# High halves of the first MLP's first weight block rounded on GpSimd instead of ScalarE

## The chip, the cores and the metric

The kernel runs on one core of a Trainium2 chip. The metric is the device time of one execution in microseconds (us), lower is better. The core has five engines that each work through their own instruction list in order: PE (TensorE, matrix products), DVE (VectorE), ACT (ScalarE), POOL (GpSimd) and SP, which here only issues DMA transfers. An engine that needs another one's result waits on a semaphore.

## The reference

Three layers follow one another. With B = 2, H = 8, S = 768, D = 64:

```python
mask = q_bucket[:, :, :, None] == k_bucket[:, :, None, :]      # 6-bit hash of q @ proj, k @ proj
scores = np.where(mask, scale * q @ k.T, -1e9)
attn = softmax(scores); x = attn @ v                           # attention, to 1536 tokens x 512
g = x @ w_gate; val = x @ w_val                                # first MLP, 512 -> 1536 -> 512
x = (silu(g) * val) @ w_out
h = x @ w_in; solu = h * softmax(h)                            # second MLP, 512 -> 1024 -> 512
out = (solu - mean) / sqrt(var + 1e-6) * g_ln @ w_out
```

The inputs are float64 for the two MLPs' weights (read as pairs of 32-bit words and turned into float32 on the chip) and the result is float32.

## The kernel before

Every matrix product is done in three products of rounded parts: a float32 number is split into a high part (a copy rounded to the matmul format, `hi`, `xh`, `eh`) and a low part (what the rounding left, `lo`, `xl`, `el`), and hi·hi, lo·hi and hi·lo are summed in PSUM.

**Attention** goes over 8 pairs of heads, 12 query slots a pair, 96 slots in all. For each slot PE computes scores (L553), DVE takes row maxima (L563), ACT the exponentials (L577), PE transposes them (L597, L595), ACT rounds the high part out of PSUM (L606), DVE makes the low part (L610), and every three slots PE multiplies with the values (L632, L636, L631). Results leave by ACT (L699, L703, or L689 for the last two), are scaled with reciprocals which POOL widens (L654, tile `wide`) and PE transposes (L665), multiplied on DVE (L714; L694 for the last), and split into `xh` and `xl` on POOL (L717, L720) or, for the last pair, on ACT and DVE (L695, L696). The scratch tiles of this step (`xf`, `low`, `both`, `wide`) live in the pool `xs`, the last SBUF pool that the attention opens.

**First MLP.** The first weight block (`w_gate` and `w_val`, 128 columns each) is brought to float32 during the attention, in `w1f[0]` and `w1f[1]`. L930 to L933, the lines of the change, split it into `hi` and `lo`. `hidden(f, blk)` then runs 24 matmuls of 512 columns per hidden block and token block (L1132); for the very first of them all 16 that use `hi` come first, the 8 that use `lo` after. The following weight blocks go through `conversions()` (L56, L58, L60, L66 or L55, L68 on DVE and ACT, then L1061 and L967), whose first five steps are traced ahead of the first matmul. 

**What sets the order.** Within the attention, and again from L1182 on, the order on each engine is the order of the code (`manual_schedule`). The lines in between, L886 to L933, are outside both: a planner places each of them in its engine's list when, by its own estimate, what it depends on is done. The planner also interleaves the two hand-ordered parts, so that matmuls of the first MLP stand in PE's list between those of the attention's last slots. The order it arrives at is fixed in the program; on the chip an engine never skips ahead in it.

**The column of ones.** `small` is a tile of 480 bytes per partition at the upper end of SBUF. Its columns hold `gl` (loaded by DMA, L888), `half` and `unit1` (memsets on DVE, L886 and L887). It is opened after the attention's pools are closed and takes memory from them: it lies at bytes 228864 to 229343 of a partition, and `wide` lies at 227616 to 229151. In the kernel before, the first users of `unit1` are the roundings of the second MLP (L1021).

Of the kernel before, what the change touches and what calls it, by code (L numbers as in the profile page):

```python
# [21 lines left out]
P = 128  # L22
# [49 lines left out]
def hash_attention_then_two_mlps(  # L72
# [16 lines left out]
    nc = tc.nc  # L89
    B, H, S, D = q.shape  # L90
    NB = proj.shape[1]
    NT, DM = out.shape
# [58 lines left out]
    w1f = [const.tile([P, DM], F32, name=f"w1f{n}") for n in range(2)]  # L151
# [724 lines left out]
    gl, half, unit1 = small[:, :KF2], small[:, KF2:KF2 + 1], small[:, KF2 + 1:KF2 + 2]  # L876
# [31 lines left out]
    with ExitStack() as m1:  # L908
# [16 lines left out]
        def weights1(f):  # L925
            hi, lo = halves(ws)
            w1_of[f] = [x.rearrange("p n (k f) -> p n k f", k=KD) for x in (hi, lo)]
            return hi, lo

        hi, lo = weights1(0)  # L930
        for n in range(2):
            nc.scalar.copy(hi[:, n], w1f[n])
            nc.gpsimd.tensor_sub(lo[:, n], w1f[n], hi[:, n].bitcast(F32))  # L933

        pieces = []
# [576 lines left out]
```

## Time and profile before

| | us |
|---|---|
| median of 3 runs | 669.58 |
| lowest, highest | 669.57, 669.98 |
| the profiled execution, its own time | 670.97 |
| its span, first to last instruction | 669.1 |
| PE busy in the span | 661.4 |
| DVE, ACT, POOL busy | 530.7, 371.5, 215.4 |

The span is 1.87 us shorter than the profiled execution's own time. "Busy" counts instructions of an engine, not its waits; "[0.56 <-DVE el L610]" behind a row of a timeline says that the engine stood idle for 0.56 us before it, until DVE's instruction of line 610 that writes `el` was done. A busy PE overlaps: a matmul's duration is longer than the distance to the next one.

### The profile page before, as it was taken

What the parts mean: (1) busy time and instruction counts of PE and PEld (TensorE: products, weight loads), DVE (VectorE), ACT (ScalarE), POOL (GpSimd) and SP (SyncE); (2) the same over time, 40 slices, a digit from 0 to 9 for tenths busy, and PEclk for the clock granted to TensorE, in tenths of its full rate; (3) what the DMA queues carried; (4) which work ended last, traced back from release to release, by engine and by line L of the source; (5) the groups of instructions that cost most, each with busy time, mean ns of one, the idle gap of its engine ahead of it and who ended that gap; (6) DMA issues with size and microseconds to landing.
All of it is one profiled execution on the core that took longest, in us unless ns stands there. A gap on an engine that the chain in (4) does not pass through costs nothing.

```text
span 669.1 us, 10300 instructions
## 1 busy us (share of the span) xinstructions
PE 661.4 (99%) x3653; PEld 578.0 (86%) x3653; DVE 530.7 (79%) x912; ACT 371.5 (56%) x754; POOL 215.4 (32%) x247
## 2 busy tenths in 40 slices
PE   8999999999999999999999999999999999999998
PEld 6999999999999988888888888888888888888887
DVE  7888899999999978957877968858974979865781
ACT  7897998989989944644234234224143533342432
POOL 6647666666626330000000000000000575776200
PEclk9999999999999999999999999999999999999999
DMA  6674754746434123351131543213014220212201
GB/s 188 171 191 118 200 147 106 184 123 168 95 93 142 48 64 119 133 189 63 64 125 64 206 171 90 99 64 119 8 63 154 71 92 36 86 69 96 94 17 48
DMA packets 39347, 73.19 MB, mean 109 GB/s; under 512 B 5336, under 2 KB 26904, under 8 KB 38528
## 3 DMA queue, kind: packets, MB, share of 16 engines
q1 hardware_dynamic: 39296, 72.53, 35.8%
q8 instruction: 29, 0.48, 0.3%
q14 instruction: 22, 0.18, 0.1%
HBM read 40.90 MB, written 7.34 MB: 72 GB/s over the span
## 4 chain that ended last, share of the span: by engine, by line
PE 93%; ACT 3%; DMA 1%; DVE 1%; issue 1%; SPq 0%; ACTq 0%; DVEq 0%
PE h L1132 29%; PE s L553 9%; PE h L1262 8%; PE t L597 5%; PE y L1160 5%; PE y L1159 5%; PE y L1158 5%; PE av L632 4%; PE av L636 4%; PE o L1374 3%; PE o L1376 3%; PE o L1375 3%; PE pp L514 2%; PE pp L475 2%; PE t L1355 1%; PE t L595 1%
## 5 line engine op out<-in xcount | busy, mean ns | idle before, releaser
L610 DVE SCALAR_TENSOR_TENSOR el<-t,eh 128x384 fp32r<-128x384 f32 x192 | 97.6, 550 | 19.1 <-ACT eh L606 18.3
L1132 PE MATMUL h<-xh,hi 128*128 128x512 f32 x288 | 112.2, 390 | 0.0
L1132 PE MATMUL h<-xl,hi 128*128 128x512 f32 x288 | 112.1, 389 | 0.0
L1132 PE MATMUL h<-xh,lo 128*128 128x512 f32 x288 | 111.2, 389 | 0.0
L606 ACT CAST eh<-t 128x384 fp32r<-128x384 f32 x192 | 84.7, 499 | 19.3 <-PE t L597 18.8
L1088 POOL TENSOR_TENSOR sf<-yh 128x256 f32<-128x256 f32 x5 | 3.7, 737 | 277.7 <-ACT yh L1173 277.7
L563 DVE TENSOR_REDUCE top<-s 128x1 f32<-128x770 f32 x96 | 90.7, 945 | 1.0 <-PE s L553 0.8
L632 PE MATMUL av<-eh,vs 128*128 128x384 f32 x186 | 64.6, 347 | 0.1
L1132 PEld LDWEIGHTS h<-xh,hi 128*128 128x128 f32 x288 | 54.1, 188 | 11.3 <-DVE sg L1142 0.2
L1132 PEld LDWEIGHTS h<-xl,hi 128*128 128x128 f32 x288 | 54.1, 188 | 11.2
L1132 PEld LDWEIGHTS h<-xh,lo 128*128 128x128 f32 x288 | 54.0, 188 | 11.2
L1142 DVE TENSOR_TENSOR sg<-h,sg 128x512 f32<-128x512 f32 x36 | 24.8, 689 | 43.3 <-PE h L1132 24.0
L553 PE MATMUL s<-ka,qa 128*128 128x384 f32 x192 | 55.1, 368 | 1.4 <-ACT e1f L577 1.2
L1061 ACT CAST hi<-wf 128x1024 fp32r<-128x1024 f32 x17 | 17.9, 1051 | 68.8 <-DVE wf L68 56.8
L1158 PE MATMUL y<-ah,hi 128*128 128x512 f32 x144 | 56.0, 389 | 0.0
L1159 PE MATMUL y<-al,hi 128*128 128x512 f32 x144 | 56.0, 389 | 0.0
L1160 PE MATMUL y<-ah,lo 128*128 128x512 f32 x144 | 56.0, 389 | 0.0
L1144 ACT CAST ah<-sg 128x512 fp32r<-128x512 f32 x36 | 22.4, 622 | 60.0 <-DVE sg L1142 60.0
L636 PE MATMUL av<-el,vs 128*128 128x384 f32 x155 | 52.3, 337 | 0.0
L553 PE MATMUL s<-kb,qb 76*128 76x384 f32 x192 | 49.4, 338 | 0.0
L1170 DVE TENSOR_TENSOR yf<-y,yf 128x512 f32<-128x512 f32 x60 | 40.2, 684 | 4.8 <-PE y L1160 4.5
L632 PEld LDWEIGHTS av<-eh,vs 128*128 128x128 f32 x186 | 35.0, 188 | 0.4 <-ACT both L703 0.4
(295 smaller groups left out, 1612.1 us busy)
## 6 DMA issues: line engine op xcount, KB each, us to landing
raw<-in_moe_w_out_dram SPq DMA_DIRECT2D x10, 1024.0 KB
raw<-in_moe_w_gate_dram SPq DMA_DIRECT2D x12, 512.0 KB
raw<-in_moe_w_val_dram SPq DMA_DIRECT2D x12, 512.0 KB
ka<-kt SPq DMA_DIRECT2D x30, 192.0 KB
raw<-in_moe_w_in_dram SPq DMA_DIRECT2D x4, 1024.0 KB
parked<-raw SPq DMA_DIRECT2D x8, 512.0 KB
moved<-u SPq DMA_DIRECT2D x8, 512.0 KB
v<-in_v_dram SPq DMA_DIRECT2D x8, 384.0 KB
```

Of the source, the lines that this page charges most:

```text
L553: nc.tensor.matmul(s[:, n, :HALF], a[:, rows], m[:, n * HALF:(n + 1) * HALF], start=first, stop=not first,)
L563: bias_of[:] = [nc.vector.tensor_reduce(tops[i % len(tops)], s_of[i][:, :, :HALF + 1], AX.XY, ALU.max, negate=True)]
L606: nc.scalar.copy(half_tile(eh_of, i, g), t_of[i, g])
L610: last_of[i] = nc.vector.scalar_tensor_tensor(half_tile(el_of, i, g), t_of.pop((i, g)), EVEN, half_tile(eh_of, i, g).bitcast(F32), ALU.add ...
L632: nc.tensor.matmul(av, vj[:, c], eh_of[h][:, c, :], start=c == 0, stop=c == C - 1)
L636: nc.tensor.matmul(*low, start=False, stop=False)
L1132: nc.tensor.matmul(ps[n], a[:, n, kk, :], x[:, kk, blk * BLK:(blk + 1) * BLK], start=kk == 0 and a is hi and x is xh, stop=kk == KD - 1 an ...
L1158: nc.tensor.matmul(p, hi[:, cols], ah, start=f == t * FT, stop=False)
L1159: nc.tensor.matmul(p, hi[:, cols], al, start=False, stop=False)
L1160: nc.tensor.matmul(p, lo[:, cols], ah, start=False, stop=f == (t + 1) * FT - 1)
L1170: nc.vector.tensor_add(y, p, y)
L1262: nc.tensor.matmul(dst, a[m](d), w3_of[b][:, l, d], start=start and n == 0, stop=n == 3 * KH - 1, skip_group_check=True,)
```

## The change

The two copies to the rounded format move from ScalarE to GpSimd, as products with a broadcast column of ones. The column is `unit1`.

```diff
         hi, lo = weights1(0)
         for n in range(2):
-            nc.scalar.copy(hi[:, n], w1f[n])
+            nc.gpsimd.tensor_mul(hi[:, n], w1f[n], unit1.to_broadcast([P, DM]))
             nc.gpsimd.tensor_sub(lo[:, n], w1f[n], hi[:, n].bitcast(F32))
```

## Rows read from the trace of the kernel before

**Rows 1.** The page: busy time by engine, and chain that ended last by engine
```profile
PE 661.4 (99%) x3653; PEld 578.0 (86%) x3653; DVE 530.7 (79%) x912; ACT 371.5 (56%) x754; POOL 215.4 (32%) x247
...
PE 93%; ACT 3%; DMA 1%; DVE 1%; issue 1%; SPq 0%; ACTq 0%; DVEq 0%
```

**Rows 2.** Busy time by stretch: length, engines (instructions), granted clock, DMA share, GB/s
```profile
204.00:206.40 2.40, 1.84 (x11) 1.42 (x9) 1.14 (x3) 2.27 (x6) 2.20 (x3) 1.00 0.11 26
206.40:231.00 24.60, 24.59 (x177) 23.80 (x178) 23.95 (x44) 23.19 (x54) 11.88 (x13) 1.00 0.34 111
...
245.73:532.00 286.27, 286.27 (x1264) 236.94 (x1264) 218.91 (x289) 113.51 (x164) 6.39 (x8) 1.00 0.30 103
```

**Rows 3.** The chain in order of time, 228 to 250: start, length, what
```profile
234.18 4.58 PE h L1132 x20
238.76 0.39 PE t L597 x5
...
239.98 0.33 PE pp L665 x3
240.31 2.98 PE h L1132 x13
243.29 0.17 PE t L632
...
245.40 0.33 PE pp L665 x3
245.73 4.36 PE h L1132 x19
```

**Rows 4.** Timeline of ACT: start, length, instruction, idle before it and what ended it
```profile
204.17 1.14 ACT L932 CAST hi<-w1f 128x512 fp32r<-128x512 f32 x2
205.22 0.85 ACT L606 CAST eh<-t 128x384 fp32r<-128x384 f32 x2
...
245.44 0.48 ACT L689 COPY low<-t 64x384 f32<-64x384 f32 x1 [3.52 <-PE t L632]
...
247.72 0.51 ACT L695 CAST xh<-xf 128x384 fp32r<-128x384 f32 x1
```

**Rows 5.** Timeline of PE at 206
```profile
206.34 0.83 PE L597 MATMUL t<-idr,e2r 128*128 128x128 f32 x5 [0.56 <-DVE el L610]
```

**Rows 6.** Timeline of DVE around the attention's end
```profile
233.55 1.03 DVE L610 SCALAR_TENSOR_TENSOR el<-t,eh 128x384 fp32r<-128x384 f32 x2 [0.62 <-ACT eh L606]
234.50 0.89 DVE L645 TENSOR_SCALAR total<-total 128x6 f32<-128x6 f32 x1
...
236.74 1.41 DVE L60 SCALAR_TENSOR_TENSOR wf<-raw,wf 128x1024 int32<-128x1024 int32 x1
...
245.94 0.55 DVE L691 TENSOR_TENSOR xf<-t,low 64x384 f32<-64x384 f32 x1 [2.98 <-ACT low L689]
246.60 0.55 DVE L694 TENSOR_TENSOR xf<-xf,pp 128x384 f32<-128x384 f32 x1
...
249.59 0.55 DVE L696 TENSOR_TENSOR xl<-xf,xh 128x384 fp32r<-128x384 f32 x1
...
250.71 0.06 DVE L887 MEMSET small<- 128x1 f32 x1
```

**Rows 7.** Instructions on the tile small: count, duration ns min/median/max, first and last start
```profile
L888 SPq DMA_DIRECT2D small<-in_moe_g_ln_dram x1: 458/458/458, 241.4 to 241.4; - x1
```

**Rows 8.** POOL's groups, shapes apart: count, busy us, mean ns, idle before them
```profile
L717 POOL TENSOR_TENSOR xh<-xf,one 128x384 fp32r<-128x384 f32 x15 | 12.4, 829 | 26.4 <-DVE top L563 21.9 <-DVE xf L714 4.5
...
L269 POOL TENSOR_TENSOR qs<-q,one 128x768 fp32r<-128x768 f32 x6 | 8.8, 1468 | 0.7 <-DVE top L563 0.7
...
L933 POOL TENSOR_TENSOR lo<-w1f,hi 128x512 fp32r<-128x512 f32 x2 | 2.6, 1290 | 0.2 <-ACT hi L932 0.2
```

**Rows 9.** Instructions on the tile wide: duration ns min/median/max
```profile
L654 POOL TENSOR_TENSOR wide<-one,r x32: 503/507/1482, 45.7 to 237.0; 128x192 f32<-128x192 f32 x32
```

**Rows 10.** Timeline of PE at the start: the seven warming matmuls, and the longest later idle time
```profile
1.22 3.17 PE L399 MATMUL t<-w1f 128*128 128x512 bf16 x7 [1.22 <-DVE w1f L172]
...
11.85 0.62 PE L553 MATMUL s<-ka,qa 128*128 128x384 f32 x2 [0.98 <-ACT e1f L577]
```

## Prediction

> **What bounds the kernel now.** I read the page first: PE is busy 661.4 of 669.1 us and 93% of the chain that ended last is PE [rows 1]. So an edit is worth what it puts into PE's list as idle time, or takes out. Next I read busy time by stretch around the place where the first weight block is used. From 206.40 to 231.00 PE is busy 24.59 of 24.60 us, and from 245.73 to 532.00 all of 286.27 us; in the 2.40 us from 204.00 it is busy 1.84 [rows 2]. Then the chain in order of time shows what fills PE at the seam between attention and first MLP: 20 matmuls of L1132 from 234.18 (4.58 us), then the transposes of the last slot, the spread L665 at 239.98, 13 more of L1132 from 240.31 (2.98 us), then the last product with the values from 243.29, the last spread, and from 245.73 only L1132 [rows 3]. These 33 matmuls, 7.56 us or 0.229 us each, are what keeps PE from waiting while the attention's last slot goes through ACT and DVE. All of them read `hi` or `lo` of the first block, or follow in PE's list matmuls that do.
>
> **The copies that go.** ACT's two casts take 1.14 us at 204.17, and the roundings of a slot (L606) stand behind them at 205.22 [rows 4]. PE then waits 0.56 us for the `el` that follows from these [rows 5]. Without the casts L606 starts about 1.1 us earlier and that wait goes. PE has no other idle time in the 24.6 us after it, so the gain should reach the end: 0.56 us. Its bounds are 0 (if another wait takes its place) and 0.56; I take 0.56.
>
> **The wait that comes.** The new products read `unit1`, and nothing before them did. `unit1` lies in memory that `wide` holds until the spread L665 that ends at 240.31 [rows 3]. So on the chip it can't be written before that matmul, whereas the casts ran at 204. In the trace the memset ran only at 250.71, behind L696, the last instruction that touches any tile of `xs`, which ends at 250.14; DVE had stood idle for 2.98 us before 245.94 [rows 6]. The DMA into another column of the same tile, a neighbour in the code, was issued at 241.4 [rows 7]. I read this so: the semaphores ask only for the tile underneath (the DMA needed no more), but the planner puts the memsets into DVE's list behind the release of the whole pool `xs`. If that is so, the order becomes: all of the attention, L696, memset, product on POOL, first L1132. PE's list can't hold an L1132 ahead of the attention's end, since the first of them needs `hi`, and the 33 covering matmuls move behind it. Queued behind that wait on PE is the whole first MLP.
>
> **The new seam, step by step.** PE has done all that is ready of the attention at 234.18 [rows 3]. The transposes of the last slot need the two L610 that end at 234.58 [rows 6], so they run at about 234.2 to 235.1 instead of 238.6. ACT rounds them by 235.9 (two L606 take 0.85 [rows 4]). DVE then makes the low parts: two L610, 1.03 us. Here I have to choose. DVE's list has L645, L56, L646, L58 and L60 in front of them now, the last of which ends at 238.15 [rows 6]. If L60 stays in front, the low parts run from 238.15 to 239.15; if the last slot overtakes the conversion, from 235.9 to 236.9. I take the first, since L56 to L60 are ready at the same time as before, and keep the second as lower bound. The last product with the values and its spread take 2.44 us (243.29 to 245.73 [rows 3]); begun when the first low part is there, at 238.7, they end at about 241.2. Behind that stands a chain of small steps: L689 0.48 and L695 0.51 on ACT [rows 4], L691, L694 and L696 0.55 each on DVE [rows 6], with some 0.2 us of handing over: 2.85 us, so L696 ends at 244.05. (In the trace it took 4.7, because the first silu and the first weights' low part were in between; neither can be there now.) The two memsets take 0.12: 244.2.
>
> **The product on POOL.** No row shows 512 columns of it. The same operation on 384 columns takes 0.829 us and on 768 columns 1.468 [rows 8]; in between that gives 0.829 + 128 x 0.639/384 = 1.04 us each, and about 0.1 to start. The first L1132 then runs at 245.3. The second product ends at 246.4; PE needs it after 8 matmuls, 1.8 us, so at 247.1: hidden. If the first subtraction (1.29 us [rows 8]) is put between the two products, PE waits some 0.6 us more; I take none. The two subtractions follow until 247.7 and 249.0; PE needs their results after 16 and 20 matmuls, at 249.0 and 249.9: hidden.
> A product on POOL can be held up: one L654 took 1.482 us where the median is 0.507 [rows 9], during a conversion on DVE; L645 took 0.89 us on six columns while POOL worked [rows 6]. I add nothing in the sum, since DVE has nothing of that kind left at 244, and 1.0 us in the upper bound.
> The Trainium skill, page "SBUF — State Buffer", section "SBUF: two separate sides", says that GpSimd and VectorE share one pair of ports as an exclusive lock and that the later one waits out the other's whole instruction. By that the product would start up to one DVE instruction later, and the two long rows agree with it.
>
> **The sum.** Before, PE at 245.73 had the attention and 33 of the matmuls behind it, so the first MLP's work stands as if it had begun without a gap at 245.73 - 7.56 = 238.17. Now it begins at 245.3: +7.1 us. From there on PE is full until 532 [rows 2], and DVE, which starts the next conversions no later against PE's place than before, has no reason to open a gap; so it all arrives at the end. Less 0.56: +6.6 us. Lower bound, the last slot overtaking the conversion: 2.6 us less, +4.0. Upper bound: the remaining conversion steps on DVE and L1061 on ACT standing in the chain of small steps (1.2 us) and POOL held up (1.0): +8.8. The profiled execution took 670.97, so a profiled one after should take 677.6; the median of the runs lies 1.39 below that execution, which gives 676.2, between 673.6 and 678.4.
>
> **The rivals.**
> *The clock falls.* PE would now have nothing from 241.4 to 245.3. The granted clock is 1.00 (2.4 GHz) in every stretch, and the longest idle times are 1.22 at the start and 0.98 later [rows 10], so no row shows what 3.9 us do. What a slow start costs is seen there too: the seven first matmuls, after no earlier work, need 0.43 us for each 512 columns (starts from 1.22 to 3.8) against 0.229, though the clock column gives 1.00 for them. Seven to eight such matmuls cost 1.5 us more: 677.7. Against it speaks that the gap is short.
> The Trainium skill, page "TensorE: Matmul & The Clock Gate", section "HAM oscillation — how this bites in real kernels", has PE fall back to half rate in pauses between bursts; it speaks against this change, and no row here can show it.
>
> *The tile alone holds the memset (not slower).* If the planner goes by `wide` and not by the pool, as the DMA's 241.4 would allow, the spread L665 runs at about 236.2, memset and product follow by 237.4, and L1132 fills PE again while the last slot is on DVE. The same 33 matmuls are then done, only later in the tail, and what is lost is 0.4 us at 234.6 and some 0.2 to 1.2 around 237, less 0.56: 669.6 to 670.6. It decides if the first L1132 starts before PE's last product with the values. For it: the DMA. Against it: the memset at 250.71, after 2.98 idle us on DVE.
>
> *The seam isn't touched.* If the ones were written early after all and the products ran at 204, where POOL is idle a third of the time, only the 0.56 us would be left: 669.0. The shared memory speaks against it.
>
> **How the numbers follow.** About 0.2% (1.3 us) is what a measurement of this kernel can tell from no change. Forecast 676.2: 0.62. Clock falls: 0.20. Tile alone: 0.12. Seam untouched: 0.05. The rest, 0.01, is a gain from a luckier order. Slower by over 0.2%: 0.62 + 0.20 + 0.02 of the tile case = 0.84. Within 0.2%: 0.14. Faster: 0.02. The range takes in the forecast's bounds and the clock case with its upper bound in part, 672.8 to 679.8; the other two, 0.17, are left out.
>
> **What would show it.** The trace after should have L886, L887 right behind L696 on DVE, at about 244; the two products on POOL at about 244.3, not at 204; no L1132 on PE before the last L665; an idle time of 3 to 5 us on PE ahead of the first L1132, ended by POOL `hi`; the transposes of the last slot at 234 to 235; and no 0.56 us wait at 206. It is wrong if L1132 still stands between the last slots on PE, or if PE shows idle time after 246 that isn't there now.

## The result

The changed kernel takes 677.23 us (median of 4 runs, 676.86 to 677.43) against 669.58 (669.33 to 669.98) before: the ratio is 1.0112, with a 95% interval of 1.0097 to 1.0127, so it is slower by 6.5 to 8.5 us. The forecast was 676.2 with a range of 672.8 to 679.8. The profiled execution of the changed kernel took 677.38 us with a span of 675.5.

The list of PE's waits of the changed kernel (us in total, times, longest) has two entries that the kernel before did not have, and the wait at 206 [rows 5] is gone. The long one is the subject here; the short one stands in the last slot, at 234.36:

```profile
PE h L1132 <- POOL hi L932: 5.7, 1, 5.7
...
PE t L632 <- DVE el L610: 0.4, 1, 0.4
```

PE's timeline (start, length, instruction, idle time before it and what ended it) shows the place. The last slot's spread is done, then PE has nothing until the first product of GpSimd is there. And the matmuls that follow start 0.43 us apart, where 0.229 was usual [rows 3]:

```profile
236.60 0.52 PE L665 MATMUL pp<-idr,wide 128*128 128x128 f32 x3
242.84 0.80 PE L1132 MATMUL h<-xh,hi 128*128 128x512 f32 x1 [5.72 <-POOL hi L932]
243.44 0.63 PE L1132 MATMUL h<-xl,hi 128*128 128x512 f32 x1
243.86 0.63 PE L1132 MATMUL h<-xh,hi 128*128 128x512 f32 x1
```

Busy time by stretch (length, then PE, PEld, DVE, ACT and POOL busy with their counts, granted clock, DMA share, GB/s) says why: the clock was granted at half, 1.2 GHz, after PE had stood idle, and for 3.6 us after it had begun again (242.84 to 246.40).

```profile
204.00:206.40 2.40, 2.40 (x19) 2.32 (x18) 2.04 (x4) 2.28 (x6) 2.02 (x2) 1.00 0.05 11
...
240.00:242.00 2.00, 0.00 (x0) 0.00 (x0) 1.08 (x5) 1.46 (x2) 1.15 (x2) 0.50 0.34 67
242.00:244.00 2.00, 1.16 (x3) 0.97 (x4) 0.00 (x0) 1.28 (x1) 2.00 (x3) 0.50 1.09 380
244.00:246.00 2.00, 2.00 (x7) 1.52 (x6) 0.00 (x0) 0.00 (x0) 2.00 (x2) 0.50 0.51 79
...
262.00:532.00 270.00, 270.00 (x1192) 223.64 (x1192) 201.69 (x264) 104.72 (x149) 1.48 (x2) 1.00 0.31 106
```

The first line answers to the 1.84 of 2.40 us before [rows 2]: the wait at 206 has gone. The last shows PE as full as before, so what happens at the seam arrives at the end. The chain in order of time (start, length, what; "issue" pieces left out but one) shows what stands between the last spread, which ends at 237.12, and the first L1132:

```profile
236.46 1.14 DVE wf L60
237.59 0.61 DVE raw L66
...
238.23 0.56 DVE xf L691
...
238.81 0.03 DVE wf L68
238.84 1.11 issue
239.95 0.56 DVE xf L694
...
240.53 0.52 ACT xh L695
...
241.08 0.56 DVE xl L696
241.64 0.01 DVE small L886
241.65 0.03 DVE small L887
...
241.75 1.05 POOL hi L932
...
242.84 19.38 PE h L1132 x77
```

**Where the time went.** The profiled execution of before lost time at its start that the other one did not: PE's last transpose L595 ahead of the copies stands at 203.85 before and at 202.73 after, and up to there the change has touched nothing. (In the experiments below it stands between 202.45 and 203.51.) So 1.12 us of the difference are chance; this is most of the 1.39 us by which the profiled execution of before lay over its median. From that landmark on:

| stretch | before | after | difference |
|---|---|---|---|
| landmark to the next transposes L597 (206.34, 204.47) | 2.49 | 1.74 | -0.75 |
| from there to the end of the values before the last slot (234.18, 231.96) | 27.84 | 27.49 | -0.35 |
| last slot by itself: before 245.73 - 234.18 less 7.56 of L1132; after 231.96 to 237.12 | 3.99 | 5.16 | +1.17 |
| PE idle ahead of L1132 | 0 | 5.72 | +5.72 |
| eight L1132 at half rate: 242.84 to 246.40, less 8 x 0.229 | 0 | 1.73 | +1.73 |

The sum is +7.52; less the chance of 1.12 it is +6.40, and the two profiled executions differ by 6.41. The medians differ by 7.65. Of the 0.35 in the second row, 0.28 belong to the wait at 206 too: its transposes took 0.66 us from L597 to L595 before (206.34 to 207.00) and 0.38 after (204.47 to 204.85). So a wait that the profile shows as 0.56 us cost about 1 us.

### The profile page after: what moved, and what is told of

The parts are those of the page before. It is cut to its first block, busy times and chain, and to the rows that moved or that the text cites. A ratio compares the mean times of both kernels' runs of the same rounds, so it can differ in the third digit from the quotient of the medians.

```text
span 675.5 us, 10299 instructions
## 1 busy us (share of the span) xinstructions
PE 662.5 (98%) x3653; PEld 578.5 (86%) x3653; DVE 530.0 (78%) x912; ACT 371.5 (55%) x752; POOL 218.8 (32%) x249
## 4 chain that ended last, share of the span: by engine, by line
PE 94%; DVE 3%; ACT 1%; issue 1%; DMA 0%; SPq 0%; POOL 0%; DVEq 0%; ACTq 0%
PE h L1132 29%; PE s L553 10%; PE h L1262 8%; PE t L597 6%; PE y L1158 5%; PE y L1160 5%; PE y L1159 5%; PE av L632 5%; PE av L636 4%; PE o L1374 3%; PE o L1376 3%; PE o L1375 3%; PE pp L514 2%; PE pp L475 2%; PE t L1355 1%; PE t L595 1%
## 5 line engine op out<-in xcount | busy, mean ns | idle before, releaser
L1132 PE MATMUL h<-xh,hi 128*128 128x512 f32 x288 | 113.2, 393 | 5.7 <-POOL hi L932 5.7
L1132 PE MATMUL h<-xl,hi 128*128 128x512 f32 x288 | 112.9, 392 | 0.0
L610 DVE SCALAR_TENSOR_TENSOR el<-t,eh 128x384 fp32r<-128x384 f32 x192 | 97.7, 550 | 17.0 <-ACT eh L606 16.1
L1132 PE MATMUL h<-xh,lo 128*128 128x512 f32 x288 | 110.9, 389 | 0.0
L1132 PEld LDWEIGHTS h<-xh,hi 128*128 128x128 f32 x288 | 54.7, 190 | 17.4 <-POOL hi L932 6.0
L1132 PEld LDWEIGHTS h<-xl,hi 128*128 128x128 f32 x288 | 54.6, 190 | 11.3
L1132 PEld LDWEIGHTS h<-xh,lo 128*128 128x128 f32 x288 | 54.1, 188 | 11.3
L553 PEld LDWEIGHTS s<-kb,qb 76*128 76x128 f32 x192 | 34.9, 189 | 0.5 <-DVE kb L441 0.5
```

Of the source, the lines that this page charges most:

```text
L553: nc.tensor.matmul(s[:, n, :HALF], a[:, rows], m[:, n * HALF:(n + 1) * HALF], start=first, stop=not first,)
L610: last_of[i] = nc.vector.scalar_tensor_tensor(half_tile(el_of, i, g), t_of.pop((i, g)), EVEN, half_tile(eh_of, i, g).bitcast(F32), ALU.add ...
L1132: nc.tensor.matmul(ps[n], a[:, n, kk, :], x[:, kk, blk * BLK:(blk + 1) * BLK], start=kk == 0 and a is hi and x is xh, stop=kk == KD - 1 an ...
```

## The experiments

The theory: `unit1` can be filled only when the whole pool `xs` has been released, so the products wait for the attention's last instruction; PE's order puts the 33 covering matmuls behind it; what is lost is the idle time and the half-rate stretch after it. The rivals: the products are dear because GpSimd makes them; or the loss comes from the new order of PE and the last slot's bare latencies; or it goes by the amount of work moved. All times are medians of runs that share a chip with runs of the kernel before:

| kernel | us | before | ratio, 95% interval |
|---|---|---|---|
| e1: ones that are there from the start | 669.94 | 669.83 | 1.0003 (0.9995 to 1.0012) |
| e2: `small` narrower | 671.51 | 669.83 | 1.0021 (1.0012 to 1.0031) |
| e3: the wait alone, work left on ScalarE | 678.57 | 669.83 | 1.0130 (1.0114 to 1.0145) |
| e4: change, gap filled with matmuls | 675.44 | 669.83 | 1.0086 (1.0072 to 1.0099) |
| e5: change, pool `xs` released earlier | 676.45 | 669.95 | 1.0098 (1.0083 to 1.0114) |
| e6: change on the second half only | 678.10 | 669.95 | 1.0124 (1.0107 to 1.0140) |
| e7: e1 with the changed kernel's order on PE | 671.45 | 669.95 | 1.0021 (1.0012 to 1.0030) |
| e8: e1 on the second half only | 669.80 | 669.95 | 0.9994 (0.9984 to 1.0004) |

"By the differences from before" means: 7.65 us for the changed kernel, and for each kernel of the table its time less that of before beside it. The intervals reach up to 1.1 us to either side, and those of e3, e4, e5 and e6 overlap that of the changed kernel. So where one of these is told apart from it by 1 or 2 us, it is the traces that carry it.

### e1: the same products without the wait

```diff
-            nc.gpsimd.tensor_mul(hi[:, n], w1f[n], unit1.to_broadcast([P, DM]))
+            nc.gpsimd.tensor_mul(hi[:, n], w1f[n], signed[:, 0:1].to_broadcast([P, DM]))
```

The first column of `signed` holds ones from the kernel's start.

> As the changed kernel, but the products read a 1.0 that lies in the attention's constant tile `signs`, written at the kernel's start. Theory (the cost is the wait for the memory under `unit1`): the products run on POOL at about 204, the 33 covering matmuls of L1132 are back between the attention's last slots, no idle time of PE ahead of them, clock 1.00 throughout; what is left is the gain on ACT, 0.56 us of PE's wait at 206 or up to 1.1: 668.5 to 669.0. Rival (the product on POOL is the cost, 1.04 us for a cast that starts every 0.57 on ACT, with POOL's later steps held up): 671 or more, no better than 669.6.

Measured: 669.94, no difference from before. The products run at 203.34 and PE's order is that of before, so the 7.65 us come from the column that is read, not from GpSimd's work. But the gain that was expected did not come either. GpSimd's timeline, with the products in the midst of attention work:

```profile
203.34 2.04 POOL L932 TENSOR_TENSOR hi<-w1f,signs 128x512 fp32r<-128x512 f32 x2 [0.60 <-PE t L595]
205.33 1.02 POOL L720 TENSOR_TENSOR xl<-xf,xh 128x384 fp32r<-128x384 f32 x1
206.30 1.47 POOL L269 TENSOR_TENSOR vs<-v,one 128x768 fp32r<-128x768 f32 x1
207.73 2.54 POOL L933 TENSOR_TENSOR lo<-w1f,hi 128x512 fp32r<-128x512 f32 x2
210.22 1.86 POOL L273 TENSOR_TENSOR vs<-v,vs 128x768 fp32r<-128x768 f32 x1
212.01 0.99 POOL L654 TENSOR_TENSOR wide<-one,r 128x192 f32<-128x192 f32 x2
```

and PE's at the end of that row:

```profile
213.06 0.55 PE L665 MATMUL pp<-idr,wide 128*128 128x128 f32 x3 [0.76 <-POOL wide L654]
```

From 203.34 to 213 GpSimd has no pause, `wide` comes out at its end, and the spread that needs it waits 0.76 us. From the landmark L595 to the transposes L597 (203.01 to 204.77) e1 is 0.73 us shorter than before, and from there to the end of the values (233.60) 0.99 longer. The wait at 206 has been moved to 213.

### e2: memory that nobody else holds

```diff
-    small = small.tile([P, 120], F32, name="small")
+    small = small.tile([P, 48], F32, name="small")
```

The columns used are fewer than 48, and a tile that narrow doesn't reach into `wide`: its 192 bytes begin at 229152, one byte behind the end of `wide`.

> As the changed kernel, but `small` is 48 columns wide instead of 120 (it uses 10), so that at the end of SBUF it no longer lies on bytes of the pool `xs`. Theory (memory under `unit1` makes the wait): the memsets go to the start of DVE's list, the products to about 204: 668.5 to 669.0, as with the constant one. Rival (the planner puts lines outside the hand-ordered parts late whatever memory they use): no change from 677.2.

Measured: 671.51, more than the 668.5 to 669.0 expected. The fills stand at the start of DVE's list (1.52 and 1.62) and the products run at 203.54, with no idle time ahead of L1132: the shared memory is what made the wait, and giving it up takes some 6 us of the loss away (7.65 and 1.68 by the differences from before). Over e1 it is 1.6 us slower by the medians, and its trace is 1.1 us longer. Some 0.2 us of that lie ahead of 532, where e2 has a new wait of 0.4 us of L514 for a transfer from `qa`; the DMA of line 888 now stands at 6.9 us in SP's list, but that it makes the wait is not shown. About 1.0 us lies behind 532: the four groups of 12 L1262 that start at 565.02, 587.12, 609.18 and 631.26 are 22.08 us apart, against 21.90 before and in e1. Why the same matmuls take longer there isn't settled; no run was made on it.

### e3: the wait without GpSimd

```diff
-            nc.scalar.copy(hi[:, n], w1f[n])
+            nc.scalar.mul(hi[:, n], w1f[n], unit1)
```

This is the kernel before, with ScalarE's copy turned into a product with `unit1`.

> The kernel before, with ACT still rounding the high parts, but as a scaling by `unit1` instead of a copy: the wait alone, without POOL's product. Theory (wait): PE idle for about 5.2 us ahead of the first L1132 (two ACT steps of 0.57 us start instead of two of 1.04 on POOL), slow first matmuls as in the changed kernel: 676.7, between 676.2 and 677.2. Rival (POOL's product is the cost): 669.6.

Measured: 678.57, above the 676.2 to 677.2 expected. The work stays on ScalarE, and the loss is there in full:

```profile
243.15 0.80 PE L1132 MATMUL h<-xh,hi 128*128 128x512 f32 x1 [5.35 <-ACT hi L932]
...
248.87 0.43 PE L1132 MATMUL h<-xl,hi 128*128 128x512 f32 x1
```

By the differences from before it is 1.1 us slower than the changed kernel. The half-rate stretch is longer: 13 matmuls instead of 8 (242.84 to 246.40 there, 243.15 to 248.87 here), 2.74 us lost instead of 1.73. The idle time is 0.37 us shorter, so from the landmark on the trace of e3 is 0.65 us the longer one; the rest of the 1.1 is within what the intervals leave open.

### e4: the gap filled

```diff
...
+                y = ps_y.tile([P, BLK], F32, tag="y", name="y")
+                with tc.issue_after(pe_last[0].ins):
+                    for _ in range(24):
+                        nc.tensor.matmul(
+                            y, xh[:, 0, :P], xh[:, 0, :BLK], start=True, stop=True
+                        )
```

24 matmuls, ordered behind the last L665, whose result nobody reads. The lines that keep the last L665 in `pe_last` are left out here.

> The changed kernel with 24 extra matmuls of 512 columns on PE, behind the attention's last one and ahead of the first L1132; their product is read by nobody. 24 x 0.229 = 5.5 us of the 5.72 us in which PE waits. Theory (the eight matmuls at 0.43 us are slow because the clock fell in the idle time): granted clock 1.00 throughout, L1132 at 0.229 from the first on, start of L1132 within 0.2 us of 242.84 in the trace: 675.5 (1.7 less than the changed kernel). Rival (they are slow for another reason, such as POOL's subtractions or the DMA burst of 380 GB/s at the same time): 677.2 or a little more.

Measured: 675.44, that is 1.79 us under the changed kernel (2.04 by the differences from before; 1.7 between the two traces, counted from the landmark). The fill does no useful work and the products come no sooner; only the clock differs. In its timeline L1135 is the fill and L1139 the first MLP's matmul:

```profile
236.64 5.73 PE L1135 MATMUL y<-xh 128*128 128x512 f32 x24
242.60 0.50 PE L1139 MATMUL h<-xh,hi 128*128 128x512 f32 x1 [0.24 <-POOL hi L933]
242.94 0.40 PE L1139 MATMUL h<-xl,hi 128*128 128x512 f32 x1
243.18 0.39 PE L1139 MATMUL h<-xh,hi 128*128 128x512 f32 x1
```

```profile
242.00:244.00 2.00, 1.76 (x8) 1.18 (x7) 0.00 (x0) 1.06 (x1) 2.00 (x3) 1.00 1.08 385
244.00:246.00 2.00, 2.00 (x11) 1.65 (x10) 0.00 (x0) 0.00 (x0) 2.00 (x2) 1.00 0.40 37
```

The clock stays at 1.00 and the matmuls are 0.23 us apart from the second on. GpSimd's subtractions and the transfers (385 GB/s) stand beside them as in the changed kernel, so the rival that these make the matmuls slow falls. Of the loss, 1.7 to 2.0 us are the clock.

### e5: the pool released earlier

```diff
-            if j == 0:
+            if j == 0 and h >= NQ - 2:
+                x_of[p, n] = [
+                    ab.tile([P, HALF], F32, tag=tag, name=name)
+                    for tag, name in (("qa", "xf"), ("qb", "low"))
+                ]
+            elif j == 0:
```

> As the changed kernel, but the two tiles of the last pair that the small chain reads and writes last (the columns that L691 to L696 work on) come out of another pool, whose memory unit1 does not touch. If the fills of small and unit1 are held by the release of the whole pool xs (theory), its last reader is now L68, not L696: the fills come some 0.85 us earlier (241.64 less the L694 and L696 that stood ahead of them), the first product with them, and the kernel takes 676.3 us (675.8 to 676.8). If the fills were held by one tile of the pool, or the wait were not what costs, nothing moves: 677.2 (676.9 to 677.5).

Measured: 676.45. By the differences from before, 1.15 us less than the changed kernel's (6.50 and 7.65); 0.78 by the medians alone. In the trace PE's idle time is 0.90 us shorter and the half-rate stretch loses 0.29 less. DVE's timeline (lines from 680 on are 5 further on: L701 is L696, L891 and L892 are the fills):

```profile
239.17 1.23 DVE L68 CUSTOM_DVE_ANT_0 wf<-raw,wf 128x2048 uint16<-128x2048 uint16 x1
...
240.35 0.06 DVE L891 MEMSET small<- 128x1 f32 x1
240.35 0.06 DVE L892 MEMSET small<- 128x1 f32 x1
241.92 0.74 DVE L701 TENSOR_TENSOR xl<-xf,xh 128x384 fp32r<-128x384 f32 x1 [1.04 <-ACT xh L700]
```

The fills no longer stand behind L696, though the tile `wide` under them and its uses are as they were. So the tile underneath alone does not order them; two tiles of the same pool that share no memory with `small` do, which is what an order by the release of the whole pool makes. That the planner goes by this release is argued, not read from the planner. What the chip itself waits for is less, and the trace shows it: the DMA into `small` (line 888, here 893), which stands ahead of the weight loads in SP's list in this run, waits at its semaphore from 230.8 and goes as soon as the spread that reads the memory under `unit1` is over, 6 us ahead of the fills into the same tile. (It is the last spread but one; the last reads a `wide` that the kernel puts in the memory of `both`.)

```profile
233.84 0.49 PE L665 MATMUL pp<-idr,wide 128*128 128x128 f32 x3
```

```profile
234.40 0.37 SPq L893 DMA_DIRECT2D small<-in_moe_g_ln_dram  x1
```

The fills, too, run before GpSimd's L720, which reads a tile of the pool, is over (241.25). PE's idle time is 4.82 us instead of 5.72. It would be less, but the product now starts only when GpSimd's L720 is out (line 725 here):

```profile
239.32 1.93 POOL L725 TENSOR_TENSOR xl<-xf,xh 128x384 fp32r<-128x384 f32 x1
241.22 2.35 POOL L937 TENSOR_TENSOR hi<-w1f,small 128x512 fp32r<-128x512 f32 x2
```

### e6: half of the change

```diff
-            nc.gpsimd.tensor_mul(hi[:, n], w1f[n], unit1.to_broadcast([P, DM]))
+            if n == 0:
+                nc.scalar.copy(hi[:, n], w1f[n])
+            else:
+                nc.gpsimd.tensor_mul(hi[:, n], w1f[n], unit1.to_broadcast([P, DM]))
```

> As the changed kernel, but only the second half of the high parts is a product on GpSimd; the first half is ScalarE's copy again. Eight of the L1132 (1.83 us) then stand ahead of the last slot's transposes. Theory: the second half still waits for the small chain behind the last spread, and that chain moves back with the last slot by what the eight take, so half of the change costs nearly the whole of it: 676.8 us (675.5 to 677.8; the low end where VectorE's conversions get done beside the eight and so leave the small chain). Rival (the loss goes by the amount of work that is moved to GpSimd): half of it, 673.4 us.

Measured: 678.10 (677.08 to 680.06), above the 675.5 to 677.8 expected: half of the work moved loses all of it (8.15 us by the differences), and the rival that goes by the amount falls. The wait is the same in a different shape. PE's waits:

```profile
PE h L1135 <- POOL hi L935: 3.8, 1, 3.8
PE t L632 <- DVE el L610: 2.0, 1, 2.0
```

Eight L1132 do cover the transposes of the last slot here, but the last low parts (L610) now stand behind the conversion in DVE's list, and the 2.0 us come from that; the clock stayed at 1.00 after it, and fell in the 3.8 us.

```profile
236.25 1.41 DVE L60 SCALAR_TENSOR_TENSOR wf<-raw,wf 128x1024 int32<-128x1024 int32 x1
237.58 0.99 DVE L66 TENSOR_SCALAR raw<-raw 128x1024 int32<-128x1024 uint32 x1
238.49 1.01 DVE L610 SCALAR_TENSOR_TENSOR el<-t,eh 128x384 fp32r<-128x384 f32 x2
```

### e7: the order on PE alone

```diff
...
             for n, kk, a, x in order:
-                nc.tensor.matmul(
+                with (tc.issue_after(pe_last[0].ins) if f == blk == 0 else ExitStack()):
+                    nc.tensor.matmul(
...
```

Upon e1: the products don't wait, but no L1132 of the first block stands ahead of the last L665. Shown is the ordering alone; the column of e1 and the lines for `pe_last` are left out.

> The products read a column of ones that is there from the start (as in e1, no wait), but every L1132 is ordered behind the last spread L665, as it came to stand in the changed kernel. It measures the lost cover of the last slot without the idle time and without the clock. The last slot by itself took 5.16 us in the changed kernel (231.96 to 237.12), and 4.16 beside L1132 in e1 (245.16 - 233.44 - 33 x 0.229). Theory: 1.0 us over e1, 670.9 (670.0 to 671.6). Rival (the loss comes from the order, with the last slot's latencies uncovered): 674 or more.

Measured: 671.45, 1.4 to 1.5 us over e1, and far from 674. In its trace the last slot stands by itself, as in the changed kernel, and takes as long as there: 5.17 us (234.05 to 239.22; 5.16 in the changed kernel).

```profile
234.05 0.85 PE L597 MATMUL t<-idr,e3r 128*128 128x128 f32 x5
...
238.70 0.52 PE L665 MATMUL pp<-idr,wide 128*128 128x128 f32 x3
```

In e1, counted as in the table above, it takes 4.00 (245.16 - 233.60 - 7.56), as before. The 4.16 that were put down ahead of the run counted from the start of the first L1132, 233.44, and not from the end of the values:

```profile
233.60 4.58 PE h L1132 x20
...
244.84 0.33 PE pp L665 x3
```

So the lost cover is 1.17 us. A further 0.48 us of the difference between the two traces lies ahead of the products, by chance (L595 of `e1f` at 203.49 and 203.01). By the runs, the order by itself costs 0.8 to 2.0 us of the 7.65.

### e8: a version that might beat both

```diff
-            nc.gpsimd.tensor_mul(hi[:, n], w1f[n], unit1.to_broadcast([P, DM]))
+            if n == 0:
+                nc.scalar.copy(hi[:, n], w1f[n])
+            else:
+                nc.gpsimd.tensor_mul(
+                    hi[:, n], w1f[n], signed[:, 0:1].to_broadcast([P, DM])
+                )
```

> A kernel that may beat both: the first half of the high parts is ScalarE's copy, the second half a product on GpSimd by a column of ones that is there from the start. GpSimd's queue behind 203 is one product (1.04 us and its issue) shorter than in e1, so L654's wide at 212 should no longer hold the spread for 0.8 us; ScalarE gives back one copy of two (half of the 0.56 us wait at 206). Theory: 669.3 us (668.8 to 669.8), against 669.8 before. If GpSimd's queue was not what ate the gain in e1, it comes out as e1: 669.9.

Measured: 669.80 against 669.95. The interval (0.9984 to 1.0004) doesn't settle a gain. The mechanism is as expected: `wide` is made at 210.46 instead of 212.01 (1.0 us sooner, counted from the landmark), and neither the wait at 206 nor that at 213 is left. From the landmark to the same place behind the seam e8 is 0.5 us shorter than before (202.46 to 243.83, and 203.85 to 245.73), which is less than these runs can tell.

```profile
208.66 1.84 POOL L273 TENSOR_TENSOR vs<-v,vs 128x768 fp32r<-128x768 f32 x1
210.46 0.97 POOL L654 TENSOR_TENSOR wide<-one,r 128x192 f32<-128x192 f32 x2
```

## Why the prediction was right, step by step

**The wait: right.** The fills are right behind L696, as forecast, and the first product 0.1 us after them. e2 shows that the memory shared with `wide` is the condition, e5 that the tile underneath alone does not set the order, which fits the release of the whole pool. e3 shows that the wait costs no less without GpSimd. The rival that the tile alone holds the memset fell with the first trace, by the sign that the prediction gave for it (the first L1132, at 242.84, stands behind PE's last product with the values, at 236.39), and again with e5; the one that the seam isn't touched fell with the first trace. One reading was right on weak ground: that the DMA needed only the tile underneath was taken from its 241.4 before. There it stood in SP's list right behind two weight loads, the first of them issued at 240.36, and did not wait at its semaphore. Only e5 shows it, at 234.40.

**Last slot: the choice was wrong.** The prediction let L60 stand ahead of the last low parts and kept the other order as lower bound. The other came: L610 at 233.79 and 234.99, L60 at 236.39. In the clock of the trace before (1.12 of chance and 1.10 of gain added), the last spread ended at 239.34, not at 241.2: 1.9 us better. The lower bound that was kept for this order is itself mis-added: by the prediction's own times the low parts come 2.25 us sooner (235.9 instead of 238.15), not 2.6. e6 is what the choice would have looked like: L60 and L66 ahead of L610, and 2.0 us of idle time.

**The chain of small steps: mis-sized.** 2.85 us were put down, 4.52 were measured (237.12 to 241.64). The conversion that had been overtaken stands in it instead: ScalarE's L689 is done at 237.25, and L60 and L66 hold L691 back to 238.23; L691 is done at 238.79, and L68 holds L694 back to 239.95. The prediction had this term in its upper bound only, as if it were independent of the choice above. It is the same work: what doesn't stand in front of the last slot stands in the chain behind it. The two errors, 1.9 and 1.7, cancel within 0.2 us; that they cancel is the shared work, that they do so this closely is luck. The idle time of PE came out longer than the 3 to 5 us that the prediction gave as a sign, 5.72, for the same reason: the last slot was done sooner, and the chain behind it took longer.

**The product: right.** 1.04 us were interpolated from 0.829 and 1.468 [rows 8]; from the fills to the first L1132 it took 1.20 (241.64 to 242.84), 1.25 were put down. The second product and the subtractions are hidden, as forecast.

**The clock: the rival came true beside the forecast.** The sum took nothing for it, and the rival had 0.20 at a price of 1.5 us. The clock fell to half, and eight matmuls lost 1.73 us; e4 gets 1.7 to 2.0 back. The 677.23 measured lie nearer to this rival's 677.7 than to the forecast's 676.2. The price came from the first matmuls of the kernel [rows 10], and it was a good one. The chance was too low: "the gap is short" was no reason, as no row of before showed a gap of that kind at all. A case that adds to the forecast should also have been added to it, and not set against it as an alternative. The Trainium skill, page "TensorE: Matmul & The Clock Gate", section "HAM oscillation — how this bites in real kernels", says that pauses between bursts of matmuls put PE back to half rate; the trace agrees, with 0.50 in the stretches from 240 to 246.

**The gain: larger than forecast.** 0.56 us were taken; from the landmark to the last slot it was 1.10 (0.75 at once, 0.35 over the next 27 us). But e1 shows that the gain holds only because the products are late: at 204 on GpSimd they cost by 213 what they gave at 206, or a little more (0.99 and 0.73). The prediction's rival of 669.0 for an untouched seam was therefore 0.9 us too good; it had left out what is queued behind the products on GpSimd.

**The sum.** 1.86 better, 1.67 worse, 0.05 better, 1.73 worse, 0.54 better: 0.95 us over the forecast; the medians say 1.03.

## What to carry to other kernels

Before a constant is used earlier than before, look where its memory lies and what the order of the program makes it wait for: here a column of ones in reused memory cost 7.65 us, and the same instruction on a column that was there from the start cost nothing that can be measured. A wait that empties PE is to be priced with the slow matmuls that follow it, and work that was overtaken is to be looked for in the chain behind. Moving work off an engine that ends a wait pays only as far as the queue that it is moved to has room before its own next deadline.

## What the runs showed of the hardware

**The clock after idle time.** After 5.72, 5.35, 4.82 and 3.76 us of idle PE (changed kernel, e3, e5, e6) the granted clock was 0.50; after 2.01 us in e6 and 0.98 before [rows 10] it was 1.00. The slow matmuls after it were 8, 13, 6 and 8, with about 0.43 us each. This number doesn't follow the idle time. Nor does the fall: in stretches of 1 us the changed kernel, idle since 237.12, has a clock of 1.00 until 239, 0.77 from 239 to 240 and 0.50 from there; e3, idle since 237.80, has 1.00 until 242 and 0.56 from 242 to 243. What sets the two is not settled here.

**GpSimd beside conversions.** L717 and L720 on 384 columns took 0.83 and 1.02 us in e1 at 201.91 and 205.33. In the changed kernel they stand beside L60, L66 and L68 on DVE:

```profile
236.54 2.35 POOL L717 TENSOR_TENSOR xh<-xf,one 128x384 fp32r<-128x384 f32 x1 [1.10 <-DVE xf L714]
238.97 1.93 POOL L720 TENSOR_TENSOR xl<-xf,xh 128x384 fp32r<-128x384 f32 x1
```

L68 runs from 238.81 to 240.04, and L720 ends 0.86 us after that, a little less than the 1.02 it takes by itself. The Trainium skill, page "SBUF — State Buffer", section "SBUF: two separate sides", says that GpSimd and some of VectorE's instructions, those with two inputs in SBUF among them, share ports which go to one instruction as a whole, and that the later one waits; these rows agree in the main. The delay cost nothing in the changed kernel, where the product starts 0.85 us after L720. In e5 it is what holds the product from 240.41 to 241.22.
